# A fused recurrent attention and soft mixture of experts: one product moved to VectorE, constants made at the beginning, and the first loads in another order

## The chip, the cores and the metric

The kernel runs on one core of a Trainium2 chip. The metric is the device time of one execution in microseconds. Three runs of the kernel before gave 171.28, 170.95 and 174.6 us, so its median is 171.28 us. Besides these there is one profiled execution, whose trace is what this document reads. TensorE (PE in the views) multiplies matrices, VectorE (DVE), ScalarE (ACT) and GpSimd (POOL) work on elements, and SyncE (SP) issues the loads and most stores. The on-chip memory is SBUF; PSUM is the small memory into which TensorE writes.

## The reference: what is computed

The first half is a gated linear attention: a running state of 48 x 48 for each of 4 x 8 heads, over 768 steps. The second half is a mixture of experts in which 32 slots are filled by softmax weights over all tokens and each token takes back a softmax mixture of the slots.

```python
# attention; B, H, S, D = 4, 8, 768, 48
f = 1.0 / (1.0 + np.exp(-f_logit))
for t in range(S):
    state = f[:, :, t, :, None] * state + np.einsum('bhd,bhe->bhde', k[:, :, t], v[:, :, t])
    y[:, :, t] = np.einsum('bhd,bhde->bhe', q[:, :, t], state)
# mixture; x is y as (3072, 384), phi (384, 32), 8 experts of 4 slots, w1 (8, 384, 1024), w2 (8, 1024, 384)
logits = x @ phi
d = softmax of logits over the tokens        # exp(logits - max) / (sum + 1e-9)
slot_input = d.T @ x
for e in range(E):
    slot_out[e] = np.maximum(slot_input[e] @ w1[e], 0.0) @ w2[e]
c = softmax of logits over the slots
out = c @ slot_out
```

## The kernel before

**Pairs.** Two heads are worked on together as a pair, one in partitions 0 to 47 and one in partitions 64 to 111. There are 16 pairs, numbered from 0; four pairs make a batch. A pair's `f`, `k` and `q` are loaded as 128 x 768 numbers (384 KB each), its `v` as 128 x 576 (288 KB). The 768 steps are cut into six chunks of 128.

**The gates of a pair.** The function `gates` enters these operations in the plan. ScalarE computes exp(-f) (`decay_exp`, L325) and ln(1 + that) (`decay_ln`, L329). VectorE adds it up along each chunk, a running sum that starts anew at each chunk (`decay_sum`, L333, tile `Lb`). ScalarE takes exp of the sum (`decay_g`, L336, tile `gb`) and of its negative (`decay_p`, L339, tile `pb`). Then `k` is multiplied with `gb` (`decay_k`, called "dk") and `q` with `pb` (`decay_q`, "dq"); both go through the helper at L342, and `es` says on which engine: 0 and 1 are GpSimd, 2 is VectorE. Pair 0 is worked on in two halves of 384 columns (`HALVES`), with both products on VectorE. Pair 1 has its product with `q` on VectorE, and its product with `k` on GpSimd. From pair 2 on, both are on GpSimd. Two small copies on GpSimd take the last column of `pb` in each chunk: `decay_pbx` ("pbx", through L316) spreads it for the state scan, `decay_pend` ("pend", L354) keeps it for a test at the end.

**The rest of a pair.** TensorE transposes `k` (`kt`, L362) and the result is copied to `kta` (L316, on ScalarE for pairs 0 and 1, on VectorE for the others). It makes the scores in two halves of three chunks (`score`, tile `sc`, L374); VectorE masks each half (L379). TensorE makes the states (`kv`, L408), VectorE runs them through the chunks (L412, tile `sb`), and TensorE adds both parts of the output up in `y` (L399, L422). ScalarE copies `y` out, TensorE makes the logits (`pl`, L454) and a transpose (`xt`, L433) one pair later. At the end of each batch the mixture's softmax adds operations on all engines, among them a division on GpSimd (`ce`, L540) and a transpose of its result on TensorE (`ct`, L546). The scores, `kt`, `y`, `xt` and `ct` share three large PSUM buffers; each is free again when the engine that reads it has copied it out.

**The constants.** `consts()` makes `same` (four copies from the identity on VectorE, L299), `consts_2()` makes `emask` (one memset of 128 x 256 and eight small ones on GpSimd, L303 and L307). `same` is first used behind the last pair, `emask` in the experts' part. Some other constants (`starts`, `mask`, `ident`, `valid`) are made ahead of the plan, at L282 to L293.

**The order.** Nothing is issued where the code stands: every operation is entered with `op(name, {engine: estimated us}, function, ..., r=reads, w=writes, due=...)`, and `Plan.run` makes one list out of them. On TensorE, ScalarE, VectorE and GpSimd the operations of the attention go strictly by `due`, the smallest first; `START` overrides the `due` of the first pairs. Loads on SyncE are not fixed in this way: at each point the one that is ready with the smallest `due` goes next, by the plan's own estimate of times. `r` and `w` set what waits for what inside the plan. The waits on the chip come from what the emitted instructions read and write. A load of weights (`lw1`, `lw2`) also gets a wait of its own, for an operation that the plan has finished by then. Each engine works through its list in order. The tail's operations are chosen by the plan too.

Of the kernel before, what the change touches and what calls it, by code (L numbers as in the profile page):

```python
# [14 lines left out]
B, H, S, D = 4, 8, 768, 48  # L15
# [39 lines left out]
def flat(t):  # L55
    n = len(t.shape)
    if n == 2:
        return t
    names = "abcde"[: n - 1]
    return t.rearrange(f"p {' '.join(names)} -> p ({' '.join(names)})")  # L60
# [9 lines left out]
class Plan:  # L70
# [22 lines left out]
    def op(self, name, engs, fn, *args, r=(), w=(), x=(), due=0.0, take=(), free=(), kb=0, home=False, ni=0):  # L93

        name, mode = name if isinstance(name, tuple) else (name, None)
        deps = set()
        for key in r:
            if key in self.writer:
                deps.add(self.writer[key])
        for key in (*w, *x):  # L100
            if key in self.writer:
                deps.add(self.writer[key])
            deps.update(self.readers.get(key, ()))
        fixed = self.fixed and "SP" not in engs
        o = Op(len(self.ops), name, engs, fn, args, due, deps, take, free, kb, home, ni, mode, fixed)
        self.ops.append(o)
        for key in w:
            self.writer[key] = o
            self.readers[key] = []
        for key in r:  # L110
            self.readers.setdefault(key, []).append(o)
        for key in (*r, *w):
            self.uses.setdefault(key, []).append(o)
        return o
# [90 lines left out]
T = 7.0  # L205
N_F, N_L, N_G, N_P, N_K, N_Q, N_V, N_SC, N_KT, N_S, N_Y = 3, 2, 2, 2, 3, 3, 4, 2, 2, 2, 3
# [4 lines left out]
def gla_soft_moe_kernel(ctx: ExitStack, tc: tile.TileContext, q, k, f, v, vt, phi, w1, w2, out):  # L211
# [11 lines left out]
    def P(shape, name, dt=F32):  # L223
        return pool.tile(shape, dt, tag=name, name=name)
# [18 lines left out]
    kb = [P([128, S], f"kb{i}") for i in range(N_K)]  # L243
    qb = [P([128, S], f"qb{i}") for i in range(N_Q)]
# [5 lines left out]
    pbx = [P([128, D, NM], f"pbx{i}") for i in range(N_S)]  # L250
# [22 lines left out]
    same = P([128, 128], "same")  # L273
    emask = P([128, 2, 4, NS], "emask")
# [20 lines left out]
    def consts():  # L295

        for g in range(4):
            gs = slice(32 * g, 32 * g + 32)
            nc.vector.tensor_copy(same[gs].rearrange("p (h s) -> p h s", h=4), ident[gs, gs].unsqueeze(1).broadcast_to([32, 4, 32]))  # L299

    def consts_2():

        nc.gpsimd.memset(emask, 0.0)  # L303
        for qq in range(4):
            for j in range(2):
                e = 2 * qq + j
                nc.gpsimd.memset(emask[:, j, qq, 4 * e : 4 * e + 4], 1.0)  # L307
# [416 lines left out]
    op = plan.op  # L724
# [4 lines left out]
    def warm(due, n, us=0.9):  # L729

        op(("warm", "square"), {"PE": us * n}, warm_up, n, due=due, take=[(("warm", due), "b")], free=[("warm", due)], ni=4 * n)

    warm(-100, 3, 1.6)
    op("consts", {"DVE": 0.5}, lambda o: consts(), w=["same"], due=30)
    op("consts_2", {"POOL": 1.0}, lambda o: consts_2(), w=["emask"], due=40)

    HALVES = (slice(0, S // 2), slice(S // 2, S))

    START = dict(
        e=(-99, -97.5), ln=(-98, -97), g=(-95.9, -95.7), p=(-95.8, -95.6),  # L740
        L=(-99, -98), dk=(-97, -95), dq=(-96, -94.5), mask=(-94.3, -92),
        kt=(-99, -96), sc=(-98, -95),
    )
    for n, (name, i) in enumerate(
# [5 lines left out]
        + [("pbx", 0), ("dk", 1), ("pend", 0)]  # L750
    ):
        START[name, i] = -80 + n
    START["e", 1], START["ln", 1], START["L", 1] = -95, -92, -94

    def load_half(o, dst, src, cs):
        nc.sync.dma_start(dst[:, cs], src[:, cs])
# [1 line left out]
    def attention(i):  # L758

        z = i * T  # L760
        F_, L_, G, PB, K, Q = (
            [(name, i % n, h) for h in range(2)]
            for name, n in (("fb", N_F), ("Lb", N_L), ("gb", N_G), ("pb", N_P), ("kb", N_K), ("qb", N_Q))
        )
        V, Y = ("vb", i % N_V), ("yT", i % N_Y)
        KT, PX, SB = ("ktb", i % N_KT), ("pbx", i % N_S), ("sb", i % N_S)
# [7 lines left out]
        else:  # L774
            op("lf", {"SP": 0.45}, load, fb[i % N_F], f[i], w=F_, due=z - (25 if i > 1 else 18.5), kb=384)
        op("lk", {"SP": 0.45}, load, kb[i % N_K], k[i], w=K, due=z - 14, kb=384)
        op("lq", {"SP": 0.45}, load, qb[i % N_Q], q[i], w=Q, due=z - 12, kb=384)
        op("lv", {"SP": 0.45}, load, flat(vb[i % N_V]), v[i], w=[V], due=z - (6 if i else 11.2), kb=288)

        def gates(cs, hs, due, n, es):  # L780

            x = len(hs) / 2
            F_h, L_h, G_h, PB_h, K_h, Q_h = ([t[h] for h in hs] for t in (F_, L_, G, PB, K, Q))
            act, dve = 0.2 + 0.72 * x, 0.06 + 1.72 * x
            by = {"POOL": 0.1 + (2.4 if i > 2 else 1.74) * x}, {"POOL": 0.1 + 1.74 * x}, {"DVE": 0.06 + 0.82 * x}
            op("e", {"ACT": act}, decay_exp, i, cs, n, r=F_h, w=[*F_h, ("esum", n)], due=due["e"])
            op("ln", {"ACT": act}, decay_ln, i, cs, r=F_h, w=F_h, due=due["ln"])
            op("L", {"DVE": dve}, decay_sum, i, cs, r=F_h, w=L_h, due=due["L"])
            op("g", {"ACT": act}, decay_g, i, cs, r=L_h, w=G_h, due=due["g"])
            op("dk", by[es[0]], decay_k, i, cs, r=[*G_h, *K_h], w=K_h, due=due["dk"])  # L790
            op("p", {"ACT": act}, decay_p, i, cs, r=L_h, w=PB_h, due=due["p"])
            op("dq", by[es[1]], decay_q, i, cs, r=[*PB_h, *Q_h], w=Q_h, due=due["dq"])

        usual = dict(e=-2 * T - 6.9, ln=-2 * T - 5.9, L=-2 * T + 2.2, g=-2 * T + 4.4, dk=-2 * T + 3.8, p=-2 * T + 4.8, dq=-2 * T + 5.6)
        if i == 0:
            for h, cs in enumerate(HALVES):
                gates(cs, [h], {name: START[name][h] for name in usual}, NP if h else 0, (2, 2))
        else:
            gates(slice(0, S), [0, 1], {name: START.get((name, i), z + t) for name, t in usual.items()}, i, (0, 2 if i == 1 else 1))
        op("pbx", {"POOL": 0.65}, decay_pbx, i, r=PB, w=[PX], due=START.get(("pbx", i), z - T + 0.7))  # L800
        op("pend", {"POOL": 0.2}, decay_pend, i, r=PB, w=[("pends", i)], due=START.get(("pend", i), z - T + 1.3))
        if i == 0:
            for h in range(2):
# [31 lines left out]
    L = B - 1  # L835
# [28 lines left out]
    for b in range(B):  # L864
        for i in range(PPB * b, PPB * b + PPB):
            first_op.append(len(plan.ops))
            attention(i)
            past_op.append(len(plan.ops))
        batch_from.append(len(plan.ops))
        if b < L:  # L870
            mixture(b, (PPB * b + PPB) * T)
# [38 lines left out]
    z = NP * T + 4  # L910
# [54 lines left out]
    for part in range(2):  # L965
# [9 lines left out]
        for u2 in range(6):  # L975
# [3 lines left out]
            for bank, (e, us) in enumerate((("ACT", 0.2 + 0.0015 * WIDE[part]), ("DVE", 0.12 + 0.0023 * WIDE[part]))):  # L979
                if (part, u2) == (1, 5):  # L980
                    e = "ACT"
# [154 lines left out]
```

## Time and profile before

| | us |
|---|---|
| median of three runs | 171.28 |
| the profiled execution's own time | 171.85 |
| its span, first to last instruction | 170.0 |
| TensorE busy in the span | 156.2 |
| VectorE busy | 115.6 |
| ScalarE busy | 94.7 |
| GpSimd busy | 89.5 |

The mean granted clock of TensorE is 0.975 of full speed. The DMA queue of SyncE moves 53.08 MB.

How to read the views: a row of the timeline gives the start and the duration in us, the engine, the line of the code, the operation, the tiles (out<-in, without their numbers), the shape, how many instructions are merged in the row, and in brackets the idle time of the engine just before and what ended it. A duration on VectorE or GpSimd includes time in which the instruction has been started but cannot proceed. A row of the waits gives the total in us, how many times, and the longest. The chain of waits is followed back from the last instruction, at each step to what released it or to the instruction before it on its engine; its rows are start, duration and what. In a row of stretches come the stretch, its length, the busy time of TensorE's matmuls, its weight loads, VectorE, ScalarE and GpSimd (with numbers of instructions), the granted clock of TensorE, the share of the DMA engines and GB/s. In the GB/s line the span is cut into 40 slices of 4.25 us.

### The profile page before, as it was taken

Reading aid. Unit: us, or ns where it says so; the run is one execution under the profiler, and the core shown is the slowest. Engines: PE = TensorE matmul, PEld = TensorE weight load, DVE = VectorE, ACT = ScalarE, POOL = GpSimd, SP = SyncE. Lnnn points to the kernel's source line nnn. Section 1 sums busy time; section 2 is a strip of 40 time slices with the busy share of each in tenths; the row PEclk is TensorE's granted clock in tenths of the full one; section 3 lists DMA queues with packets and bytes.
Section 4 is the critical chain, followed back from the end, with each engine's and each line's share of the span. In section 5 each row is a group of like instructions: output and inputs, shape, how many; then the busy total and the mean of one; then the engine's idle time right before and its main releaser. Section 6 shows DMA issues by size and latency. Waiting matters only on the chain.

```text
span 170.0 us, 6026 instructions
## 1 busy us (share of the span) xinstructions
PE 156.2 (92%) x2546; PEld 121.6 (72%) x2546; DVE 115.6 (68%) x167; ACT 94.7 (56%) x169; POOL 89.5 (53%) x88
## 2 busy tenths in 40 slices
PE   5999989999899999999998999999899999989850
PEld 2477778988788959889896989888554454568640
DVE  2899959889989985898996989746540234134420
ACT  5799696875777759679674782541421211042330
POOL 3109999886589895897896988741000001000000
PEclk9999999999999999999999999999999999999955
DMA  5999999999999999999987569999999790009892
GB/s 153 333 407 371 390 399 397 395 400 397 393 381 394 386 382 401 396 401 392 393 301 192 169 178 274 367 404 401 394 401 363 241 325 16 2 4 381 319 354 80
DMA packets 20468, 54.08 MB, mean 318 GB/s; under 512 B 2272, under 2 KB 2640, under 8 KB 20432
## 3 DMA queue, kind: packets, MB, share of 16 engines
q1 hardware_dynamic: 20144, 53.08, 84.6%
q8 instruction: 22, 0.36, 0.9%
q10 hardware_dynamic: 288, 0.52, 0.9%
q14 instruction: 14, 0.11, 0.2%
HBM read 48.87 MB, written 4.72 MB: 315 GB/s over the span
## 4 chain that ended last, share of the span: by engine, by line
PE 54%; POOL 16%; DVE 9%; DMA 6%; issue 6%; ACT 4%; SPq 1%; POOLq 0%; ACTq 0%; DVEq 0%
PE sc L374 9%; PE y L399 7%; PE up L620 6%; POOL qb L342 5%; PE y L422 4%; POOL kb L342 4%; PE kv L408 4%; PE kt L362 4%; PE xt L433 4%; PE pf L712 3%; DMA fb<-in_f_dram 3%; POOL pbx L316 3%; PE po L666 3%; DVE Lb L333 3%; PE pl L454 3%
## 5 line engine op out<-in xcount | busy, mean ns | idle before, releaser
L342 POOL TENSOR_TENSOR kb<-kb,gb 112x768 f32<-112x768 f32 x15 | 27.5, 1832 | 18.0 <-ACT gb L336 14.6
L333 DVE TENSOR_TENSOR_SCAN Lb<-starts,fb 112x768 f32<-112x768 f32 (+1 forms) x17 | 34.3, 2018 | 2.8 <-ACT fb L329 2.6
L379 DVE TENSOR_TENSOR scb<-sc,mask 128x768 f32<-128x768 f32 x32 | 29.2, 950 | 4.9 <-PE sc L374 4.8
L374 PE MATMUL sc<-qb,kb 48*128 48x128 f32 x384 | 26.3, 281 | 1.4 <-DVE kta L316 0.8
L316 POOL COPY pbx<-pb 112x240 f32<-112x240 f32 x16 | 24.5, 1533 | 5.4 <-ACT pb L339 5.4
L342 POOL TENSOR_TENSOR qb<-qb,pb 112x768 f32<-112x768 f32 x14 | 27.0, 1930 | 0.0
L399 PE MATMUL y<-scb,va 128*48 128x128 f32 (+1 forms) x384 | 26.0, 276 | 0.1
L374 PEld LDWEIGHTS sc<-qb,kb 48*128 48x128 f32 x384 | 22.9, 187 | 4.3 <-DVE kta L316 1.0
L316 ACT COPY yT<-y 112x768 f32<-112x768 f32 x16 | 12.8, 799 | 20.4 <-PE y L422 20.4
L399 PEld LDWEIGHTS y<-scb,va 128*48 128x48 f32 (+1 forms) x384 | 21.9, 130 | 1.0 <-DVE scb L379 0.7
L540 POOL TENSOR_TENSOR ce<-ce,cm 128x256 f32<-128x256 f32 x4 | 4.7, 1170 | 29.3 <-DVE cm L537 29.3
L336 ACT ACTIVATE gb<-Lb 112x768 f32<-112x768 f32 (+1 forms) x17 | 13.7, 806 | 6.7 <-DVE Lb L333 6.7
L316 DVE COPY kta<-kt 128x672 f32<-128x672 f32 x14 | 11.9, 847 | 7.8 <-PE kt L362 7.8
L329 ACT ACTIVATE fb<-fb,one 112x768 f32<-112x768 f32 (+1 forms) x17 | 15.3, 898 | 0.6
L325 ACT ACTIVATE fb<-fb 112x768 f32<-112x768 f32 (+1 forms) x17 | 13.7, 806 | 1.8 <-DMA fb<-in_f_dram 1.8
L422 PE MATMUL y<-qb,sb 48*48 48x128 f32 x320 | 14.6, 285 | 0.0
L408 PE MATMUL kv<-va,kta 128*64 128x48 f32 (+1 forms) x384 | 14.4, 220 | 0.0
L408 PEld LDWEIGHTS kv<-va,kta 128*64 128x64 f32 (+1 forms) x384 | 12.4, 130 | 2.6 <-ACT kta L316 0.8
L362 PE MATMUL kt<-ident,kb 112*128 112x112 f32 x96 | 13.1, 270 | 0.5 <-POOL kb L342 0.2
L339 ACT ACTIVATE pb<-Lb 112x768 f32<-112x768 f32 (+1 forms) x17 | 13.5, 794 | 0.0
L422 PEld LDWEIGHTS y<-qb,sb 48*48 48x48 f32 x320 | 11.1, 162 | 2.7 <-DVE sb L412 2.6
L362 PEld LDWEIGHTS kt<-ident,kb 112*128 112x128 f32 x96 | 9.9, 142 | 3.0 <-DVE kb L342 1.2
(154 smaller groups left out, 261.1 us busy)
## 6 DMA issues: line engine op xcount, KB each, us to landing
w1a<-in_w_dram SPq DMA_DIRECT2D x34, 384.0 KB, 6.7
kb<-in_k_dram SPq DMA_DIRECT2D x16, 384.0 KB, 6.7
qb<-in_q_dram SPq DMA_DIRECT2D x16, 384.0 KB, 6.7
fb<-in_f_dram SPq DMA_DIRECT2D x15, 384.0 KB, 6.2
va<-in_v_dram SPq DMA_DIRECT2D x16, 288.0 KB, 6.4
out_dram<-w1a SPq DMA_DIRECT2D x6, 512.0 KB, 3.8
scb<-in_w_dram SPq DMA_DIRECT2D x4, 384.0 KB, 6.8
fb<-in_w_dram SPq DMA_DIRECT2D x3, 384.0 KB, 4.1
```

Source lines behind the costliest of these rows:

```text
L316: {"ACT": nc.scalar.copy, "DVE": nc.vector.tensor_copy, "POOL": nc.gpsimd.tensor_copy}[o.eng](dst, src)
L325: nc.scalar.activation(t, t, AF.Exp, scale=-1.0, accum_out=esum[:, n : n + 1])
L329: nc.scalar.activation(t, t, AF.Ln, bias=one[:PW])
L333: nc.vector.tensor_tensor_scan(Lb[i % N_L][:PW, cs], flat(starts)[:PW, cs], fb[i % N_F][:PW, cs], 0.0, op0=ALU.mult, op1=ALU.add)
L336: nc.scalar.activation(gb[i % N_G][:PW, cs], Lb[i % N_L][:PW, cs], AF.Exp)
L342: (nc.vector if o.eng == "DVE" else nc.gpsimd).tensor_tensor(t, t, by, op=ALU.mult)
L362: nc.tensor.transpose(u[:, C * m : C * m + PW], kb[i % N_K][:PW, C * m : C * m + C], ident[:PW, :PW])
L374: nc.tensor.matmul(u[:, 512 * r + C * m : 512 * r + C * m + C], kb[i % N_K][rs, cs], qb[i % N_Q][rs, cs], start=True, stop=True,)
L379: nc.vector.tensor_tensor(scb[i % N_SC][:, :, h], un["sc", i, h].rearrange("p (r x) -> p r x", r=2)[:, :, : 3 * C].rearrange("p r (m t) -> ...
L399: nc.tensor.matmul(u[rows(at), y_cols(m)], va[:, v0 : v0 + (D if at else 64)], scb[i % N_SC][:, r, h, m % 3], start=m % 3 == 0, stop=False ...
L408: nc.tensor.matmul(u[rows(r), :, m], ktb[i % N_KT][:, m, rows(r)], vb[i % N_V][:, m, r], start=True, stop=True)
L422: nc.tensor.matmul(u[at : at + D, y_cols(m)], sb[i % N_S][rs, :, m - 1], qb[i % N_Q][rs, C * m : C * m + C], start=False, stop=m in (2, 5) ...
```

## The change

Five edits in the planning code; the operations themselves stay as they are.

- The constants `same` and `emask` get a `due` of -110, the smallest on their engines, so that they come ahead of all attention work on VectorE and GpSimd.
- The load of `q` of pair 0 is entered as two loads of 384 columns (192 KB each), due -12 and -11.3. The load of `f` of pair 1 is due 7 - 18.5 = -11.5 and thus stands between the two. `v` of pair 0 is due -11.2.
- The product of pair 2 with `q` goes from GpSimd to VectorE (`es` is now (0, 2) for pair 2 too).
- Its `due` is 8.5, by a new entry of `START`; by the rule for the usual pairs it was 5.6. On VectorE the state scan of pair 1 is due 8.2 and the running sum of pair 3 is due 9.2, so it stands between those.
- `pbx` of pair 0 is entered as reading `q` of pair 0 too. In the plan it thereby follows the product of pair 0 with `q`; the copy itself reads `pb` alone.

```diff
-    op("consts", {"DVE": 0.5}, lambda o: consts(), w=["same"], due=30)
-    op("consts_2", {"POOL": 1.0}, lambda o: consts_2(), w=["emask"], due=40)
+    op("consts", {"DVE": 0.5}, lambda o: consts(), w=["same"], due=-110)
+    op("consts_2", {"POOL": 1.0}, lambda o: consts_2(), w=["emask"], due=-110)
...
-    START["e", 1], START["ln", 1], START["L", 1] = -95, -92, -94
+    START["e", 1], START["ln", 1], START["L", 1], START["dq", 2] = -95, -92, -94, 8.5
...
-        op("lq", {"SP": 0.45}, load, qb[i % N_Q], q[i], w=Q, due=z - 12, kb=384)
+        if i == 0:
+
+            for h, cs in enumerate(HALVES):
+                op("lq", {"SP": 0.45}, load_half, qb[0], q[0], cs, w=Q[h : h + 1], due=-12 + 0.7 * h, kb=192)
+        else:
+            op("lq", {"SP": 0.45}, load, qb[i % N_Q], q[i], w=Q, due=z - 12, kb=384)
...
-            gates(slice(0, S), [0, 1], {name: START.get((name, i), z + t) for name, t in usual.items()}, i, (0, 2 if i == 1 else 1))
-        op("pbx", {"POOL": 0.65}, decay_pbx, i, r=PB, w=[PX], due=START.get(("pbx", i), z - T + 0.7))
+            gates(slice(0, S), [0, 1], {name: START.get((name, i), z + t) for name, t in usual.items()}, i, (0, 2 if i in (1, 2) else 1))
+        op("pbx", {"POOL": 0.65}, decay_pbx, i, r=PB if i else [*PB, *Q], w=[PX], due=START.get(("pbx", i), z - T + 0.7))
```

## The prediction, made before the result was known

> **What bounds the kernel now.** Pairs, halves and loads are numbered from 0: the change's "first q" is q of pair 0, "second f" that of pair 1, "third product" pair 2's. I read the page first, then the waits of TensorE.
>
> ```profile
> span 170.0 us, 6026 instructions
> GB/s 153 333 407 371 390 399 397 395 400 397 393 381 394 386 382 401 396 401 392 393 301 192 169 178 274 367 404 401 394 401 363 241 325 16 2 4 381 319 354 80
> PE 54%; POOL 16%; DVE 9%; DMA 6%; issue 6%; ACT 4%; SPq 1%; POOLq 0%; ACTq 0%; DVEq 0%
> ```
> ```profile
> PE ct L546 <- POOL ce L540: 1.5, 3, 0.6
> PE sc L374 <- DVE kta L316: 0.8, 1, 0.8
> PE sc L374 <- POOL qb L342: 0.4, 1, 0.4
> ```
>
> The profiled execution took 171.85 us, 1.85 around its span of 170.0, and lies 0.57 above the median of 171.28. The chain that ended last is mostly TensorE, with GpSimd and VectorE next, so the few places where TensorE waits are what an edit can win. The timeline of TensorE says when:
>
> ```profile
> 23.39 1.61 PE L374 MATMUL sc<-qb,kb 48*128 48x128 f32 x24 [0.40 <-POOL qb L342]
> 29.70 1.61 PE L374 MATMUL sc<-qb,kb 48*128 48x128 f32 x24
> 42.30 0.94 PE L374 MATMUL sc<-qb,kb 48*128 48x128 f32 x12
> 44.09 0.94 PE L374 MATMUL sc<-qb,kb 48*128 48x128 f32 x12 [0.85 <-DVE kta L316]
> 63.80 0.44 PE L546 MATMUL ct<-ident,ce 128*128 128x128 f32 x2 [0.45 <-POOL ce L540]
> ```
>
> From the scores of pair 2 (23.39) to those of pair 5 (42.30) a pair costs TensorE (42.30 - 29.70) / 2 = 6.30 us without a hole; before 23.39 the start sets the time; behind it there are a hole of 0.85 in pair 5 and one of 0.45 at the first ct. A gain before 44 reaches the end only if no later wait grows.
>
> **The port.** These rows of VectorE, GpSimd and ScalarE carry the prices:
>
> ```profile
> 13.00 1.84 POOL L342 TENSOR_TENSOR kb<-kb,gb 112x768 f32<-112x768 f32 x1 [4.54 <-ACT gb L336]
> 13.68 1.97 DVE L342 TENSOR_TENSOR qb<-qb,pb 112x768 f32<-112x768 f32 x1
> 18.27 1.83 POOL L342 TENSOR_TENSOR kb<-kb,gb 112x768 f32<-112x768 f32 x1 [0.42 <-ACT gb L336]
> 19.79 1.93 DVE L333 TENSOR_TENSOR_SCAN Lb<-starts,fb 112x768 f32<-112x768 f32 x1
> 20.07 3.27 POOL L342 TENSOR_TENSOR qb<-qb,pb 112x768 f32<-112x768 f32 x1
> 22.45 0.86 DVE L316 COPY kta<-kt 128x672 f32<-128x672 f32 x1 [0.74 <-PE kt L362]
> 23.35 0.83 ACT L336 ACTIVATE gb<-Lb 112x768 f32<-112x768 f32 x1
> 29.42 0.83 DVE L316 COPY kta<-kt 128x672 f32<-128x672 f32 x1
> ```
>
> GpSimd's product with g ran 13.00 to 14.84. VectorE's product with q was begun at 13.68 and ended at 15.65, which is 0.81 after GpSimd was done: it waited. The other way round, GpSimd's product of 20.07 took 3.27 instead of 1.83, since the running sum on VectorE lasted until 21.72. I read these as one shared access to SBUF that a two-input operation of either engine holds to its end; a full product then costs 0.81 on VectorE and 1.83 on GpSimd.
>
> **Part 1, the start.** The chain of waits, then the timeline:
>
> ```profile
> 2.17 0.43 SPq L320
> 2.64 5.67 DMA fb<-in_f_dram
> 9.31 0.94 ACT fb L329
> ```
> ```profile
> 7.45 0.56 DVE L342 TENSOR_TENSOR qb<-qb,pb 112x384 f32<-112x384 f32 x1 [0.48 <-DMA qb<-in_q_dram]
> 7.64 0.82 POOL L316 COPY pbx<-pb 112x240 f32<-112x240 f32 x1 [5.39 <-ACT pb L339]
> 7.93 0.95 DVE L342 TENSOR_TENSOR kb<-kb,gb 112x384 f32<-112x384 f32 x1
> 8.34 0.85 ACT L325 ACTIVATE fb<-fb 112x768 f32<-112x768 f32 x1 [0.84 <-DMA fb<-in_f_dram]
> 8.80 0.55 DVE L342 TENSOR_TENSOR qb<-qb,pb 112x384 f32<-112x384 f32 x1
> 9.27 0.95 DVE L379 TENSOR_TENSOR scb<-sc,mask 128x768 f32<-128x768 f32 x1
> 10.28 1.76 DVE L333 TENSOR_TENSOR_SCAN Lb<-starts,fb 112x768 f32<-112x768 f32 x1
> ```
>
> f of pair 1 lands at 2.64 + 5.67 = 8.31, with ScalarE idle for 0.84. Half of q is 192 KB, 0.197 MB; taken from before f it frees 0.197 / 333 GB/s = 0.59 us of the loads, so f lands near 7.72 and ln ends near 10.25 - 0.59 = 9.66. The first product with q loses its 0.48 wait (6.97 to 7.52), and the product with k follows it (to 8.05). But the second half of q now lands where f did, 8.31, and GpSimd's copy of the chunk ends has the port meanwhile: its 0.82 from 7.64 overlaps the first q product until 8.01, so it needs 0.45, and from 8.05 it holds until 8.50. Product 8.50 to 9.05, mask to 10.0 at most (each row above starts some 0.06 before the one ahead ends, which makes it 9.9). So the running sum of pair 1 starts at 9.9, not 10.28: 0.4 us. Behind it g, the product with g (13.00), the product with q (13.68) and the next sum follow in a line of waits, so the 0.4 reaches 23.39 whole. Ends: 0 (second half late) and 0.59. The extra load costs SP one issue of 0.43, behind which v of pair 0 and all later loads are queued; those loads wait for data, not for SP, and I count nothing.
>
> The chunk ends "behind" q: the new entry orders the plan, while the copy itself reads only p, so it may well start at 7.64 as before. If it does move behind the second q product, that product starts at 8.31 rather than 8.50: 0 to 0.2 us, inside the ends above.
>
> **Part 2, pair 2's product on VectorE.** GpSimd loses 3.27 (20.07 to 23.34); VectorE gains 0.81, between the state scan and the sum of pair 3. Both are 0.4 earlier: the product with g on GpSimd ends at 20.10 - 0.4 = 19.7 and holds the port until then, so the new product runs 19.7 to 20.5 and the sum of pair 3, queued behind it, 20.5 to 22.2 (21.72 before). Behind that sum are the copy of kt (22.45, now 22.2) and, on ScalarE, g of pair 3. But 23.35 shows no idle time before that g: ScalarE is busy until then, so the later sum costs it nothing. TensorE's wait of 0.40 at 23.39 goes. What is late next: g of pair 3, GpSimd's two products, the sum of pair 4 and the kt copy of 29.42, which are no earlier than the start made them. That copy ends at 30.25, and the second half of the scores that takes its PSUM buffer is due at 29.70 + 0.77 = 30.47. The margin is 0.22 less the signalling, so of the 0.40 about 0.1 stays. Pair 2's copy of the chunk ends now stands directly behind the product with g on GpSimd; if it takes the port at 19.7 first, the new product, the sum and the kt copy come 0.45 later, and that copy ends at 23.5 where the second half of the scores is due at 23.39 - 0.8 + 0.77 = 23.36: then the wait of TensorE only changes its name. Ends: 0 and 0.4.
>
> **Part 3, the constants.**
>
> ```profile
> 4.41 0.96 DVE L333 TENSOR_TENSOR_SCAN Lb<-starts,fb 112x384 f32<-112x384 f32 x1 [2.38 <-ACT fb L329]
> 38.56 1.83 POOL L342 TENSOR_TENSOR qb<-qb,pb 112x768 f32<-112x768 f32 x1
> 39.39 2.11 DVE L299 COPY same<-ident 32x128 f32<-32x128 f32 x4
> 41.53 1.76 DVE L333 TENSOR_TENSOR_SCAN Lb<-starts,fb 112x768 f32<-112x768 f32 x1
> 43.20 0.83 DVE L316 COPY kta<-kt 128x672 f32<-128x672 f32 x1
> 52.32 0.33 POOL L303 MEMSET emask<- 128x256 f32 x1
> ```
>
> The four copies wait for the port until 40.39 and then keep the sum of pair 6 from it until 41.53, so 1.14 is lost; the kt copy behind it comes at 43.20 and TensorE waits 0.85 for it. Without them the sum runs 40.39 to 42.1 and the copy ends at 42.9, when the first half of the scores (42.30 + 0.77 = 43.07) is not over: the whole 0.85 goes. At the beginning they stand in front of the sum of 4.41, before which VectorE is idle 2.38; even at the 2.11 measured with the port taken they fit. The emask writes meet an idle GpSimd (5.39 before 7.64). Where they are now, they delay products that TensorE has not waited for: nothing in itself.
>
> The first ct:
>
> ```profile
> 61.54 1.79 DVE L333 TENSOR_TENSOR_SCAN Lb<-starts,fb 112x768 f32<-112x768 f32 x1
> 61.76 1.98 POOL L540 TENSOR_TENSOR ce<-ce,cm 128x256 f32<-128x256 f32 x1
> ```
>
> GpSimd's ce waits for a sum that took the port 0.2 before it; both come behind small operations whose start is tied to TensorE. With GpSimd earlier (no emask, no 1.14) those wait less: 0.2 of the 0.45 goes; ends 0 and 0.45.
>
> **Sum.** 0.4 + 0.1 + 0.85 + 0.2 = 1.55 us. The profiled time becomes 171.85 - 1.55 = 170.3, the median 171.28 - 1.55 = 169.7. With all ends against it, 0.85 (170.4); with all for it, 0.59 + 0.4 + 0.85 + 0.45 = 2.3 (169.0). The likeliest case's own range is 169.0 to 170.4. Chance 0.62.
>
> **Rivals.** *No gain at the start* (0.18): halves land no sooner, because each load has a price of its own and the second half of q makes VectorE late. In the rows above loads of the start do not arrive at an even rate (333 GB/s in the second slice, 407 in the third), which leaves this open; it takes 0.4 off the sum: 170.1. In the Trainium skill, "DMA: Bandwidth & Descriptors", section "Rules for kernel authors" asks for transfers of 1 MiB or more and its anatomy section gives each a fixed 2.0 us on GpSimd's path; added in full this would make it 171.28 - 1.55 + 2.0 = 171.7, an estimate. No run here shows that price; the deep queue of 5.67 us before f lands speaks against its being serial, and I give it 0.03 of the 0.18.
>
> *The loads set the pace* (0.09): from 4 to 85 us the loads run near 390 GB/s, and a kernel 1.55 ahead could meet them: 171.3. Against: after 8.34 no TensorE wait above names a load, and in slices 21 to 24 (301 down to 169 GB/s) there is room before the last weights.
>
> *Slower* (0.07): the clock of TensorE falls earlier in the ending.
>
> ```profile
> 159.29 1.27 PE L712 MATMUL pf<-pin,cT 32*128 32x128 f32 x24 [0.43 <-ACT pin L316]
> 160.93 2.72 PE L712 MATMUL pf<-pin,cT 32*128 32x128 f32 x24 [0.37 <-DVE w1a L316]
> 161.50:162.00 0.50, 0.50 (x8) 0.43 (x6) 0.04 (x1) 0.31 (x1) 0.00 (x0) 0.52 0.82 328
> ```
>
> The granted clock falls to half at 161.5; the same 24 matmuls then take 2.72 instead of 1.27, at most 1.45 more (some of it is waiting for buffers). If the fall comes one group earlier, at 159.3 or before, another 1.45 is lost and the gain is nearly gone (171.2); two groups earlier, the time is 169.7 + 2.9 = 172.6, which is this rival. It turns the sign once over 1.55 us are added by matmuls at half clock. For: the ending shifts in time, and TensorE waits there often. Against: the ending's instructions are the same. "TensorE: Matmul & The Clock Gate", section "What's actually happening" of the Trainium skill has the clock set by free-running windows of about 3.4 us of activity; this trace shows the fall with waits of only 0.4 near it and cannot show the windows.
>
> The rest, 0.04, is a plan that comes out different behind 65 us, to either side by 2% or more.
>
> **Numbers.** 169.7 is the likeliest. The range takes in its ends, the lost start and no gain: 168.9 to 171.4, with the later clock fall and the plan's surprises outside. 2% is about what a measurement here can tell from no change; it begins at 167.9 and 174.7, which only the last case reaches: faster 0.03, slower 0.02, same 0.95.
>
> **What would show it.** Right: f of pair 1 landed by 7.8 and the sum of pair 1 at 9.9; "same" copied before 4.4; a VectorE product with q near 19.7 of about 0.8; no wait of TensorE on kta in pair 5 or on qb in pair 2; the ct of 63.80 some 1.5 earlier, its wait about 0.25. Wrong: a sum of pair 1 still at 10.2 (part 1), a kt copy that TensorE waits for in pair 3 or 4 (part 2), a ct wait over 0.45 or a load among TensorE's releasers (rivals), a granted clock of 0.5 before 159 (the slower case).

## The result and the profile after

The changed kernel takes 169.50 us (median of four runs, 169.17 to 169.71) against 171.60 us (median of four runs, 170.95 to 174.6) of the kernel before, measured again beside it: a ratio of 0.9876, 95% interval 0.9851 to 0.9902. The run of 174.6 is of a slower state that some executions show, and the ratios here leave such runs out. The interval leaves out 1, although the change is smaller than the 2% that the prediction took as about what a measurement here can tell. The gain is 2.1 us, where 1.55 had been forecast; the forecast time of 169.7 was 0.2 too high. A second measurement of the same kernel gave 169.42 us and 0.988, interval 0.9847 to 0.9913. The profiled execution took 169.48 us with a span of 167.7, so its own difference is 171.85 - 169.48 = 2.37 us.

The page of the kernel after: span, GB/s per slice, and the shares of the chain that ended last by engine.

```profile
span 167.7 us, 6030 instructions
GB/s 127 350 410 368 391 394 399 397 401 396 394 392 393 400 396 398 398 395 401 394 357 259 125 212 337 314 402 401 396 399 361 229 324 30 2 4 388 315 359 88
PE 64%; DVE 12%; DMA 5%; POOL 5%; issue 4%; ACT 3%; SPq 1%; ACTq 0%; POOLq 0%; DVEq 0%
```

GpSimd's share of the chain fell from 16% to 5%, TensorE's rose from 54% to 64%. What is left, in the view of TensorE's waits after, of the three lines that the prediction began with:

```profile
PE ct L546 <- POOL ce L540: 1.0, 2, 0.6
PE sc L374 <- DVE kta L316: 0.4, 1, 0.4
```

The wait on `qb` is no longer there, that on `kta` is half as long (and in another pair, as the timeline shows), and one of the three on `ce` has gone. No load is among TensorE's releasers. The same places in TensorE's timeline after:

```profile
14.35 0.79 PE L362 MATMUL kt<-ident,kb 112*128 112x112 f32 x6 [0.23 <-POOL kb L342]
21.95 0.94 PE L374 MATMUL sc<-qb,kb 48*128 48x128 f32 x12
23.26 0.94 PE L374 MATMUL sc<-qb,kb 48*128 48x128 f32 x12 [0.36 <-DVE kta L316]
28.89 1.80 PE L374 MATMUL sc<-qb,kb 48*128 48x128 f32 x24
35.38 1.61 PE L374 MATMUL sc<-qb,kb 48*128 48x128 f32 x24
41.78 1.61 PE L374 MATMUL sc<-qb,kb 48*128 48x128 f32 x24
43.31 0.84 PE L408 MATMUL kv<-va,kta 128*64 128x48 f32 x23
48.41 1.61 PE L374 MATMUL sc<-qb,kb 48*128 48x128 f32 x24
61.73 0.44 PE L546 MATMUL ct<-ident,ce 128*128 128x128 f32 x2
89.98 0.44 PE L546 MATMUL ct<-ident,ce 128*128 128x128 f32 x2 [0.59 <-POOL ce L540]
119.01 0.33 PE L472 MATMUL te<-ident,et 128*128 128x128 f32 x1 [0.53 <-ACT et L467]
```

These are `kt` of pair 1, the scores of pairs 2 (in two halves), 3, 4 and 5, the states of pair 5 (`kv`), the scores of pair 6, the first and second `ct`, and a transpose `te` late in the attention. The wait inside pair 2 is now for its kt copy instead of its `q`; the hole in pair 5 is closed. Three rows of the kernel before that the prediction does not show:

```profile
14.89 0.79 PE L362 MATMUL kt<-ident,kb 112*128 112x112 f32 x6 [0.24 <-POOL kb L342]
50.05 1.61 PE L374 MATMUL sc<-qb,kb 48*128 48x128 f32 x24
121.08 0.33 PE L472 MATMUL te<-ident,et 128*128 128x128 f32 x1 [0.53 <-ACT et L467]
```

Cutting both timelines at the same instructions gives a sum that can be followed, and the experiments below are read by the same cuts (all in us, "from ... to" between the starts):

| | before | after | gain |
|---|---|---|---|
| start of `kt` of pair 1 | 14.89 | 14.35 | 0.54 |
| from there to the scores of pair 5 | 27.41 | 27.43 | -0.02 |
| from there to the scores of pair 6 | 7.75 | 6.63 | 1.12 |
| from there to the first `ct` | 13.75 | 13.32 | 0.43 |
| from there to the `te` above | 57.28 | 57.28 | 0.00 |
| from there to the end of the span | 48.92 | 48.69 | 0.23 |

The gain up to `te` is 2.07 us: the start and the constants have all of it, and the stretch that holds pair 2's product has none.

### The profile page after: what moved, and what is told of

It reads as the page before. It is cut to its first block, busy times and chain, and to the rows that moved or that the text cites. A ratio compares the mean times of both kernels' runs of the same rounds, so it can differ in the third digit from the quotient of the medians.

```text
span 167.7 us, 6030 instructions
## 1 busy us (share of the span) xinstructions
PE 154.7 (92%) x2546; PEld 120.5 (72%) x2546; DVE 115.5 (69%) x168; ACT 94.9 (57%) x169; POOL 90.0 (54%) x87
## 4 chain that ended last, share of the span: by engine, by line
PE 64%; DVE 12%; DMA 5%; POOL 5%; issue 4%; ACT 3%; SPq 1%; ACTq 0%; POOLq 0%; DVEq 0%
PE sc L374 11%; PE y L399 10%; PE up L620 7%; PE y L422 6%; PE kv L408 6%; PE kt L362 5%; DVE Lb L333 5%; PE xt L433 5%; PE pl L454 3%; PE po L666 3%; DMA qb<-in_q_dram 3%; PE pf L712 3%; DMA out_dram<-w1a 2%; POOL ce L540 2%; DVE scb L379 2%
## 5 line engine op out<-in xcount | busy, mean ns | idle before, releaser
L316 POOL COPY pbx<-pb 112x240 f32<-112x240 f32 x16 | 26.8, 1676 | 4.7 <-ACT pb L339 4.7
L342 POOL TENSOR_TENSOR qb<-qb,pb 112x768 f32<-112x768 f32 x13 | 23.8, 1828 | 0.0
L412 DVE TENSOR_TENSOR_SCAN sb<-kv,pbx 112x288 f32<-112x288 f32 x16 | 11.9, 747 | 0.2 <-issue 0.2
```

Of the source, the lines that this page charges most:

```text
L316: {"ACT": nc.scalar.copy, "DVE": nc.vector.tensor_copy, "POOL": nc.gpsimd.tensor_copy}[o.eng](dst, src)
L342: (nc.vector if o.eng == "DVE" else nc.gpsimd).tensor_tensor(t, t, by, op=ALU.mult)
```

## The experiments

The theory after the result: each row of that table belongs to one edit, and pair 2's product is worth nothing because something behind it has a pace of its own. The rival: the product on VectorE is what lets the earlier start through.

**The constants alone.** The kernel before with the two entries changed:

```diff
-    op("consts", {"DVE": 0.5}, lambda o: consts(), w=["same"], due=30)
-    op("consts_2", {"POOL": 1.0}, lambda o: consts_2(), w=["emask"], due=40)
+    op("consts", {"DVE": 0.5}, lambda o: consts(), w=["same"], due=-110)
+    op("consts_2", {"POOL": 1.0}, lambda o: consts_2(), w=["emask"], due=-110)
```

> The kernel before with only the constants made at the beginning. Theory (the changed kernel's gains are separate and sit in stages): kt of pair 1 stays at 14.89 us, the scores of pair 5 at 42.3, TensorE's wait for kta in pair 5 is gone and the scores of pair 6 come at 48.95 instead of 50.05 (1.1 less), the first ct's wait of 0.45 goes too; the time falls by 1.4 to 1.6 us, ratio near 0.991. Rival (the wait is worth what its row says, and the ct wait belongs to the start): 0.85 less, the ct wait stays at 0.4, ratio 0.995.

Measured: 170.33 us, ratio 0.9896, interval 0.9831 to 0.9961. The cuts are 14.76, 27.41, 6.63 and 13.32: the third and fourth are exactly those of the changed kernel, the first and second those of the kernel before within 0.13. So the constants give 1.12 + 0.43 = 1.55 us, and nothing else is needed for it.

**The two constants apart.** Each is one of the two entries, on the kernel before.

> The kernel before with only the four copies for the constant 'same' made at the beginning; emask stays among the products. Theory: from the scores of pair 5 to those of pair 6 it takes 6.63 us instead of 7.75, since this part belongs to the copies alone; from there to the first ct 13.6 to 13.75 instead of the 13.32 that both constants gave, since emask keeps GpSimd late. Rival (the ct wait went because of the copies): 13.32.

> The kernel before with only emask written at the beginning; the copies stay in front of the sum of pair 6. Theory: scores of pair 5 to scores of pair 6 stay at 7.75 us with the wait of 0.85 for kta; from there to the first ct 13.3 to 13.5 instead of 13.75. Rival (emask costs nothing anywhere): 13.75.

With `same` early (one run, 170.53 us, span 168.7) the cuts are 6.64 and 13.57; with `emask` early (one run, 171.6 us, span 169.7) they are 7.75 and 13.53. TensorE's rows of the second:

```profile
43.92 0.94 PE L374 MATMUL sc<-qb,kb 48*128 48x128 f32 x12 [0.85 <-DVE kta L316]
63.41 0.44 PE L546 MATMUL ct<-ident,ce 128*128 128x128 f32 x2 [0.32 <-POOL ce L540]
```

The hole in pair 5 is therefore the copies' alone; the gain of 0.43 at the first `ct` is 0.18 from the copies and 0.22 from the memsets.

**The loads alone.** `q` of pair 0 in halves around `f` of pair 1, and the entry for the chunk ends:

```diff
-        op("lq", {"SP": 0.45}, load, qb[i % N_Q], q[i], w=Q, due=z - 12, kb=384)
+        if i == 0:
+
+            for h, cs in enumerate(HALVES):
+                op("lq", {"SP": 0.45}, load_half, qb[0], q[0], cs, w=Q[h : h + 1], due=-12 + 0.7 * h, kb=192)
+        else:
+            op("lq", {"SP": 0.45}, load, qb[i % N_Q], q[i], w=Q, due=z - 12, kb=384)
...
-        op("pbx", {"POOL": 0.65}, decay_pbx, i, r=PB, w=[PX], due=START.get(("pbx", i), z - T + 0.7))
+        op("pbx", {"POOL": 0.65}, decay_pbx, i, r=PB if i else [*PB, *Q], w=[PX], due=START.get(("pbx", i), z - T + 0.7))
```

> The kernel before with only the first q in halves around the second pair's f (and the chunk ends entered as behind q). Theory: the running sum of pair 1 starts at 9.76 instead of 10.28, kt of pair 1 at 14.35; the whole 0.5 stays through pair 5 (scores at 41.8), the kta wait of 0.85 and the ct wait of 0.45 stay as they were; the time falls by 0.5 us, ratio 0.997. Rival (a later wait takes it): the scores of pair 6 or the first ct are where they were, ratio 1.000.

The first measurement gave no ratio, as two of its four runs were far off (219 and 296 us); it was repeated.

> The kernel before with only the first q in halves around the second pair's f, once more. Theory: scores of pair 5 about 0.5 earlier than in executions of the old order of loads, 27.4 us behind kt of pair 1 as in all others; 7.75 from there to the scores of pair 6; the time 0.3 to 0.5 us below before, ratio 0.997 to 0.998. Rival: no difference, ratio 1.000.

Measured: 171.45 us, ratio 0.9987, interval 0.9949 to 1.0025; 0.4 us would be 0.9977, so the time neither shows nor excludes it. In the profiles of the two measurements `kt` of pair 1 begins at 14.72 and 14.44, and the other three cuts are those of the kernel before (27.40, 7.75, 13.75 and 13.73).

One such start proves little, since the start differs from execution to execution. Over all profiles here but that of the next experiment, the five with the old loads have `kt` of pair 1 at 14.72, 14.76, 14.81, 14.89 and 15.26, mean 14.89; the eight with the new ones at 14.21, 14.27, 14.30, 14.35, 14.44, 14.57, 14.72 and 14.97, mean 14.48. That is a gain of 0.41 on average, with a 95% interval of about 0.1 to 0.7: there is a gain, and its size is known only roughly. What varies is above all the landing of `f` of pair 1. With the old loads ScalarE waits for it in all five profiles (0.49 to 0.97 us). With the new ones it waits in three of the eight (0.45, 0.80 and 0.45), and these have the three latest starts (14.72, 14.97 and 14.57); in the other five it does not wait.

**Both halves ahead of `f`.** The rival for the start was that cutting the load in two is what helps, wherever the halves stand. The kernel of the loads alone, with both halves issued first:

```diff
-                op("lq", {"SP": 0.45}, load_half, qb[0], q[0], cs, w=Q[h : h + 1], due=-12 + 0.7 * h, kb=192)
+                op("lq", {"SP": 0.45}, load_half, qb[0], q[0], cs, w=Q[h : h + 1], due=-12 + 0.4 * h, kb=192)
```

> The first q in halves, but both ahead of the second pair's f; the rest as before. Theory (the start is gained by f being loaded earlier): f lands at 8.2 to 8.7 as before, the running sum of pair 1 starts at 10.1 to 10.4 although the first product with q starts earlier. Rival (it is the first half of q that frees VectorE): the sum of pair 1 starts at 9.7 to 9.8.

Measured in one run: 171.74 us, span 170.1. ScalarE and VectorE of this kernel:

```profile
8.82 0.84 ACT L325 ACTIVATE fb<-fb 112x768 f32<-112x768 f32 x1 [1.09 <-DMA fb<-in_f_dram]
10.76 1.76 DVE L333 TENSOR_TENSOR_SCAN Lb<-starts,fb 112x768 f32<-112x768 f32 x1 [0.87 <-ACT fb L329]
```

The first product with `q` runs at 7.13, with no wait, as in the changed kernel. But ScalarE waits 1.09 for `f`, VectorE 0.87 for ScalarE, and `kt` of pair 1 begins at 15.37, later than in any of those. So halves alone do not help; as far as one execution can show it, it is the place of `f` that counts.

**The product alone, and the change without it.** Edits 3 and 4 on the kernel before, and taken out of the changed kernel:

```diff
-    START["e", 1], START["ln", 1], START["L", 1] = -95, -92, -94
+    START["e", 1], START["ln", 1], START["L", 1], START["dq", 2] = -95, -92, -94, 8.5
...
-            gates(slice(0, S), [0, 1], {name: START.get((name, i), z + t) for name, t in usual.items()}, i, (0, 2 if i == 1 else 1))
+            gates(slice(0, S), [0, 1], {name: START.get((name, i), z + t) for name, t in usual.items()}, i, (0, 2 if i in (1, 2) else 1))
```

> The kernel before with only the third pair's product with q on VectorE. Theory: the scores of pair 2 begin about 0.8 earlier than 23.39, but the kt copies of pairs 3 and 4 end where they did, so the scores of pair 5 stand at 42.3 again and the time does not change, ratio 1.000. Rival (the wait of 0.40 is saved for good): scores of pair 5 at 41.9, ratio 0.9975.

> The changed kernel with the third pair's product with q left on GpSimd. Theory: the same time as the changed kernel (ratio to before 0.988), with scores of pair 2 near 22.85, of pair 5 at 41.8 and of pair 6 at 48.4. Rival (that product is worth 0.4 us): 0.4 slower than the changed kernel, ratio 0.990, scores of pair 6 at 48.8.

Alone: 172.29 us, ratio 1.0024, interval 0.9982 to 1.0067, with cuts of 15.26, 27.33, 7.82 and 13.94; the last three add up to 0.18 more than before. Left out: 169.32 us, ratio 0.9858, interval 0.981 to 0.9906, with 14.27, 27.41, 6.63 and 13.33. So the change is as good without this product, and the rival falls: the earlier start comes through without it. The rows of GpSimd and ScalarE say why; first the kernel without the product on VectorE:

```profile
19.44 3.28 POOL L342 TENSOR_TENSOR qb<-qb,pb 112x768 f32<-112x768 f32 x1
22.73 0.83 ACT L336 ACTIVATE gb<-Lb 112x768 f32<-112x768 f32 x1
23.64 1.83 POOL L342 TENSOR_TENSOR kb<-kb,gb 112x768 f32<-112x768 f32 x1 [0.25 <-ACT gb L336]
```

and the changed kernel:

```profile
22.81 0.83 ACT L336 ACTIVATE gb<-Lb 112x768 f32<-112x768 f32 x1
23.72 1.83 POOL L342 TENSOR_TENSOR kb<-kb,gb 112x768 f32<-112x768 f32 x1 [1.28 <-ACT gb L336]
25.52 1.81 POOL L342 TENSOR_TENSOR qb<-qb,pb 112x768 f32<-112x768 f32 x1
29.96 1.84 POOL L342 TENSOR_TENSOR kb<-kb,gb 112x768 f32<-112x768 f32 x1 [0.49 <-ACT gb L336]
```

`g` of pair 3 begins 22.73 - 14.27 = 8.46 behind `kt` of pair 1 without the product and 22.81 - 14.35 = 8.46 with it, both times with no idle time before it: ScalarE's own list sets it. The product with `g` begins 9.37 behind in both. The 3.28 us that GpSimd was relieved of came back as waiting: 1.28 us for `g` instead of 0.25, and 1.34 and 1.66 us for the two small copies between (shown further down) instead of 0.61 and 0.20. From there on a loop runs with a period of 29.96 - 23.72 = 6.24: two products on GpSimd, the next running sum on VectorE, which needs the port that they hold, then `g`. TensorE, at 6.30 for a pair, is bound by hardly more. The scores of pair 2, now 21.95 - 14.35 = 7.60 behind `kt` of pair 1 instead of 23.39 - 14.89 = 8.50, are 0.90 earlier, and the three pairs from there to 41.78 take 19.83 instead of 18.91. This goes in two steps, as the scores of pairs 2 to 5 show: counted from `kt` of pair 1, they are 0.90, 0.27, 0.08 and -0.02 earlier than before. The first 0.63 is lost inside pair 2, to its own kt copy, which comes late behind the running sum (its rows are further down). Only the other 0.29 is left for the loop to take.

**Pair 3's product on VectorE as well.** If that loop holds pairs 3 to 5, taking one product out of it must release something:

```diff
-    START["e", 1], START["ln", 1], START["L", 1], START["dq", 2] = -95, -92, -94, 8.5
+    START["e", 1], START["ln", 1], START["L", 1], START["dq", 2], START["dq", 3] = -95, -92, -94, 8.5, 15.5
...
-            gates(... (0, 2 if i in (1, 2) else 1))
+            gates(... (0, 2 if i in (1, 2, 3) else 1))
```

> The changed kernel with the fourth pair's product with q on VectorE too, behind the state scan of pair 2. Theory (in pairs 3 to 5 the kt copy is held by the port, which a product holds 1.83 us from GpSimd and 0.81 from VectorE): TensorE keeps 0.2 to 0.3 of what it has gained by pair 2, the scores of pair 5 come 27.15 us behind kt of pair 1 instead of 27.4, and the time falls by 0.25 more, ratio to before 0.986. Rival (another operation holds the kt copy): 27.4 as in all kernels so far, no gain.

Measured: 170.31 us, ratio 0.9904, interval 0.9874 to 0.9935, not distinguishable from the changed kernel; the 0.986 that was expected lies outside. In the trace, TensorE and VectorE, with one row of VectorE in the changed kernel last:

```profile
22.57 0.94 PE L374 MATMUL sc<-qb,kb 48*128 48x128 f32 x12
29.51 1.61 PE L374 MATMUL sc<-qb,kb 48*128 48x128 f32 x24
26.44 1.11 DVE L342 TENSOR_TENSOR qb<-qb,pb 112x768 f32<-112x768 f32 x1
27.47 1.75 DVE L333 TENSOR_TENSOR_SCAN Lb<-starts,fb 112x768 f32<-112x768 f32 x1
29.14 0.83 DVE L316 COPY kta<-kt 128x672 f32<-128x672 f32 x1
```
```profile
28.87 0.83 DVE L316 COPY kta<-kt 128x672 f32<-128x672 f32 x1
```

The kt copy is 29.14 - 14.97 = 14.17 behind `kt` of pair 1 (28.87 - 14.35 = 14.52 in the changed kernel, 29.42 - 14.89 = 14.53 in the kernel before), and the second cut falls from 27.43 to 27.15. So the loop is shown as the holder in pairs 3 to 5, at a price of 0.28. It is not the whole answer: the scores of pair 3 still come 29.51 - 22.57 = 6.94 behind those of pair 2, as in the changed kernel (28.89 - 21.95), where a pair without a hole takes 6.30. That part, the kt copy of pair 2, was not taken away in any experiment. Up to `te` 0.23 of the 0.28 is left (104.43 behind `kt` of pair 1 instead of 104.66). The profiled execution began late (14.97) and took 50.5 us from `te` to its end, against 48.6 to 49.2 in all others, although TensorE's last matmuls begin 39.85 behind `te` as in the changed kernel (39.84); so its time says little about the edit.

**The quotient on VectorE.** What is left in the waits after is `ct` on GpSimd's `ce`. One more edit moves that small product to VectorE, ahead of the running sum:

```diff
-        nc.gpsimd.tensor_tensor(ce, ce, cm.unsqueeze(2).broadcast_to([128, 8, NS]), op=ALU.mult)
+        (nc.vector if o.eng == "DVE" else nc.gpsimd).tensor_tensor(ce, ce, cm.unsqueeze(2).broadcast_to([128, 8, NS]), op=ALU.mult)
...
-        op("cdiv", {"POOL": 0.55}, c_div, r=["ce", "cm"], w=["ce"], due=z[0] + 5.9)
+        op("cdiv", {"DVE": 0.4}, c_div, r=["ce", "cm"], w=["ce"], due=z[0] + 5.25)
```

First with pair 3's product on VectorE too, beside a repetition of the changed kernel; then by itself on the changed kernel.

> The changed kernel with the fourth pair's product with q on VectorE and, in each batch, the division of ce on VectorE behind the sum that it needs, in front of the next running sum. Theory: GpSimd's ce waits for a running sum that holds the port; on VectorE it takes about 0.4 us, so TensorE's waits for ce (0.59 at the second ct, 0.4 in the last batch) go; time 0.8 to 1.2 us below the changed kernel, ratio to before 0.981. Rival (the running sum, now 0.4 later, makes a kt copy late): the gain is nothing.

> The changed kernel beside the two above: ratio to before 0.988, scores of pair 5 27.4 us behind kt of pair 1, 6.63 to those of pair 6, 13.32 to the first ct.

> The changed kernel with the quotient ce of each f computed on VectorE, in front of the pair's running sum, in place of GpSimd; pair 3's product with q stays as the changed kernel has it. Theory (the chunk-end transposes still wait for GpSimd's quotient, 0.59 us at the second of them and about 0.4 at the last batch, and nothing else waits for it): both waits go from TensorE's timeline, pair 5's scores stay 27.4 us behind pair 1's key transposes because the port loop is untouched, the transpose te of the ending begins 0.8 to 1.0 us earlier measured from pair 1's key transposes than in the changed kernel, and the time is 168.4 to 168.9, ratio about 0.984. Rival: VectorE's 0.42 us in front of each running sum makes a kt copy or a product late by as much; the waits go and come back at the scores, and the ratio stays at 0.988.

With both: 168.77 us, ratio 0.983, interval 0.9785 to 0.9874. The quotient alone: 168.68 us, ratio 0.9809, interval 0.977 to 0.9848. Its runs lie at 168.05 to 169.26, the eight of the changed kernel at 169.17 to 169.71. Its view of the waits and its rows at the first two `ct`:

```profile
PE ct L546 <- DVE ce L540: 0.2, 1, 0.2
```
```profile
59.85 0.42 DVE L540 TENSOR_TENSOR ce<-ce,cm 128x256 f32<-128x256 f32 x1
60.19 1.75 DVE L333 TENSOR_TENSOR_SCAN Lb<-starts,fb 112x768 f32<-112x768 f32 x1
62.84 0.86 DVE L316 COPY kta<-kt 128x672 f32<-128x672 f32 x1 [0.90 <-PE kt L362]
61.79 0.44 PE L546 MATMUL ct<-ident,ce 128*128 128x128 f32 x2
89.38 0.44 PE L546 MATMUL ct<-ident,ce 128*128 128x128 f32 x2
118.40 0.33 PE L472 MATMUL te<-ident,et 128*128 128x128 f32 x1 [0.53 <-ACT et L467]
```

The same product in the changed kernel, with the sum that stood ahead of it:

```profile
59.52 1.75 DVE L333 TENSOR_TENSOR_SCAN Lb<-starts,fb 112x768 f32<-112x768 f32 x1
59.75 1.93 POOL L540 TENSOR_TENSOR ce<-ce,cm 128x256 f32<-128x256 f32 x1 [0.48 <-PE y L422]
```

On GpSimd it took 1.93, and ended 0.41 behind the sum; on VectorE it takes 0.42 and goes first. The first `ct` is 13.14 behind the scores of pair 6 instead of 13.32, the second 89.38 - 61.79 = 27.59 behind the first instead of 28.25, and `te` is 103.83 behind `kt` of pair 1 (14.57) instead of 104.66: 0.83 us. The 0.4 in front of the sum cost nothing: the next kt copy, at 62.84, still waits 0.90 for TensorE. The version with both has `te` at 117.83 - 14.30 = 103.53, another 0.30 less. Its median of 168.77 holds one run of 171.15; the other five lie at 167.78 to 169.45 with a median of 168.16. These two versions are the fastest here, and the times don't tell which of them is faster.

The fifth edit, the chunk ends of pair 0 entered as reading `q`, was not run by itself: without it every engine gets the same list of instructions. The copy of the changed kernel starts at 7.73, when `p` of the second half is done.

## Why the prediction came near

**The start: right in size as far as it is known, and its steps held but for one landing.** The chain and the timelines after:

```profile
3.12 5.04 DMA qb<-in_q_dram
```
```profile
7.67 0.84 ACT L325 ACTIVATE fb<-fb 112x768 f32<-112x768 f32 x1
8.25 0.71 DVE L342 TENSOR_TENSOR qb<-qb,pb 112x384 f32<-112x384 f32 x1 [0.17 <-DMA qb<-in_q_dram]
9.76 1.74 DVE L333 TENSOR_TENSOR_SCAN Lb<-starts,fb 112x768 f32<-112x768 f32 x1
```

ScalarE does not wait for `f` in this execution. The second half of `q` landed at 3.12 + 5.04 = 8.16, 0.15 ahead of the 8.31 forecast, and now gates, as forecast; the sum began at 9.76 instead of 9.9. The 0.4 of the sum measures 0.54 between these two executions and 0.41 between the means; that the mean comes so close is partly chance, since its interval is 0.1 to 0.7. The rival *no gain at the start* fell with it. It had the Trainium skill's "DMA: Bandwidth & Descriptors" beside it ("Rules for kernel authors": transfers of 1 MiB or more; a fixed 2.0 us for each on GpSimd's path in its anatomy section). With a full 2.0 us, an estimate from that page's figure, the loads alone would have given (171.55 - 0.41 + 2.0) / 171.55 = 1.009; the interval ends at 1.0025, so the measurement decides against adding that price for one more queued load.

**The third pair's product: right that next to nothing stays, 0.1 forecast, 0 measured.** Each link was named; who would get the port, only the trace after could show. VectorE after, then GpSimd:

```profile
19.07 1.30 DVE L342 TENSOR_TENSOR qb<-qb,pb 112x768 f32<-112x768 f32 x1
20.29 2.16 DVE L333 TENSOR_TENSOR_SCAN Lb<-starts,fb 112x768 f32<-112x768 f32 x1
22.38 0.82 DVE L316 COPY kta<-kt 128x672 f32<-128x672 f32 x1
```
```profile
19.50 1.34 POOL L316 COPY pbx<-pb 112x240 f32<-112x240 f32 x1
20.78 1.66 POOL L354 COPY pends<-pb 112x6 f32<-112x6 f32 x1
```

The copy of the chunk ends did get the port, but between the product and the sum rather than ahead of both: the sum takes 2.16 where the one at 9.76 above took 1.74. The kt copy came as late as the prediction feared, and TensorE's wait of 0.40 on `qb` became 0.36 on `kta`. "The wait of TensorE only changes its name" is what happened. The 0.40 itself was too small: the scores of pair 2 moved by 0.90, and the wait on `qb` shows as 0.83 in the kernel without the product, where they stand at the same 8.50 behind `kt` of pair 1 (22.77 - 14.27). The step that failed is "of the 0.40 about 0.1 stays": it took the margin of one kt copy, that of 29.42. In pair 4 0.08 is indeed left, and it is gone by pair 5, since the product with `g` of pair 3 holds all that follows. The prediction had that operation in its list of what is late next.

The small copy of 112 x 6 took 1.66 us against 0.19 at 17.12 and 29.27, and ended at 22.44, with the sum (22.45): it had to wait the sum out. The Trainium skill says of this in "SBUF — State Buffer" (section on who interferes with whom) that VectorE and GpSimd share one pair of ports as an exclusive lock for a whole instruction, and that the loser blocks; the trace agrees, also for plain copies of GpSimd.

**The constants: right mechanism, a term too small.** The 0.85 was read from the idle time in TensorE's row, and 1.12 came. The 0.2 at the first `ct` was 0.43; its upper end was 0.45. "Nothing in itself" does not hold for the `emask` writes: moved alone they gave 0.22 there. In the kernel before, this row follows the two halves of pair 5's scores (42.30 and 44.09, in the prediction); beside them are to be laid the scores of 41.78 and the `kv` of 43.31 after:

```profile
44.96 0.84 PE L408 MATMUL kv<-va,kta 128*64 128x48 f32 x23
```

From the first score to the first `kv` it was 2.66 and is 1.53: 1.13 lost, 0.28 more than the idle time. The row's idle time begins where the first half is taken to end, 42.30 + 0.94 = 43.24, while the second half would have begun 0.77 behind the first, at 43.07; that is 0.17 of it. The other 0.11 is that the second half itself took 0.87 to the next operation instead of 0.77. The prediction had the 0.77 and used it to say that the hole would close; it did not use it for the hole's size. The Trainium skill warns of this in "Perfetto Trace Analysis", in its part on the life of a TensorE instruction: the end that the profiler gives for a matmul is computed from its size, not observed. This case gives the warning a price. The same holds for the wait of 0.59 at the second `ct`, whose removal gave 0.66, and for the first `ct` after, which shows no wait and yet came 0.18 earlier without GpSimd.

**The constants' new place** was covered, as forecast. VectorE after:

```profile
1.93 1.17 DVE L299 COPY same<-ident 32x128 f32<-32x128 f32 x4
4.59 0.96 DVE L333 TENSOR_TENSOR_SCAN Lb<-starts,fb 112x384 f32<-112x384 f32 x1 [1.49 <-ACT fb L329]
```

The copies took 1.17 instead of 2.11, and VectorE still waits 1.49 before its first sum.

**The other rivals.** *The loads set the pace* did not come, although a load now takes 7.3 to 7.6 us from issue to landing (6.2 to 6.7 before): nothing on TensorE waits for one. *Slower, by the clock* did not come, and its price finds no support. TensorE's last rows and the stretch in which the clock fell, after:

```profile
158.85 1.80 PE L712 MATMUL pf<-pin,cT 32*128 32x128 f32 x24 [0.37 <-DVE w1a L316]
163.50:164.00 0.50, 0.00 (x0) 0.00 (x0) 0.00 (x0) 0.00 (x0) 0.00 (x0) 0.80 1.03 381
```

The fall came near 163.8, behind the last matmuls, and these took 1.80 instead of 2.72. Yet the end is only 0.23 closer to `te` than before, where the rival's price would give 0.92. In the profiles where the last 24 matmuls met the lower clock the stretch from `te` to the end was 48.70, 48.92 and 49.01, in those where they did not 48.57 to 49.17 (the 50.5 above aside). The stores, at 381 GB/s in the row above, may be what sets the end there; this was not tested. The windows in "TensorE: Matmul & The Clock Gate", section "What's actually happening", of the Trainium skill can't be seen in these profiles either.

**The sum.** Forecast 0.4 + 0.1 + 0.85 + 0.2 = 1.55; measured to `te` 0.54 - 0.02 + 1.12 + 0.43 = 2.07. The forecast time came nearer than the sum by chance: it started from a median of 171.28, and the kernel before stood at 171.6 beside the changed one.

## What to carry to other kernels

Take the size of a hole on TensorE from start to start, against the same instructions where nothing waits; the idle time in a row begins at a computed end and was 0.07 to 0.28 us short here. Before moving an operation off a loaded engine, find the next operation of that engine and ask what sets it: here the 3.28 us taken from GpSimd became waiting, because ScalarE's list set the next product, and the small copies between waited for the port. Work that nobody needs for a long time, such as constants, belongs where its engine waits anyway; in the middle of a chain around a shared port, 2.11 us of small copies cost over 1 us.

## What was unexpected of the hardware

The start of a profile, up to `kt` of pair 1, varied by 0.54 us among five executions with the same order of loads (14.72 to 15.26) and by 0.76 among eight with the other, as much as the gain itself; edits at the start need several profiles. The granted clock did not fall at a fixed place of the program: it fell 40.4 us behind `te` in the kernel before (161.5), 44.8 in the changed one (163.8), and 42.5 and 40.9 with `same` alone and `emask` alone moved, though TensorE's work from `te` on is the same in all. And TensorE's last matmuls at half clock, 0.9 us longer, left no mark on the end that could be told from the scatter.
